# Loading v and z as fp32 through SyncE's queue and casting them on chip, in a gated attention and hypermixer kernel

## The chip, the cores and the metric

The kernel runs on one core of one Trainium2 chip. The metric is the device time of one execution in microseconds; a kernel is timed in several runs, and the median is given. A profiled execution of its own gives the trace and the page of views.

## The reference

Two stages follow each other, for 8 batches of 3200 rows:

```python
# u, v: (8, 3200, 256); z: (8, 3200, 64); w_q, w_k: (256, 64); w_out: (256, 256)
scores = (1.0 / S) * np.matmul(z, z.transpose(0, 2, 1))
attn = np.maximum(scores, 0.0) ** 2
x = u * np.matmul(attn, v)                       # the first stage
wq, wk = x @ w_q, x @ w_k                        # the second stage
W_tok = (1.0 / np.sqrt(64)) * np.einsum('bsd,btd->bst', wq, wk)
mixed = np.einsum('bst,btd->bsd', W_tok, x)
out = np.maximum(mixed, 0.0) @ w_out
```

All inputs and the output are fp32. The kernel multiplies in fp16.

## The kernel before, in words

**Tiling.** A batch is 25 blocks of 128 rows. The output rows of a batch are taken in seven groups (six of 512 rows and one of 128, `widths`). For each group and each of the 25 blocks, the scores are a 128 x 512 matrix: PE multiplies z with z (L263), two of these matrices making a pair in two PSUM banks (tile `sc`). A first stage on ACT or DVE takes the positive part into an fp32 tile `g` (`first_stage`, L286 and L290); a second stage on ACT or POOL squares it into the fp16 tile `at` (`second_stage`, L306 and L308). PE then multiplies `at` with the rows of v and adds up the group's output in four PSUM accumulators (`second_product`, tile `acc`, L351). At a group's end the two halves of the accumulators are added (L368, L369), multiplied with u on POOL (L388, tile `x_sb`) and transposed by a DMA (tile `xT_sb`).

**Symmetry.** The scores are symmetric, so a block that lies near the diagonal is computed once and its transposed copy is made by a DMA transpose from `at` into the tiles `tt` and `ttl` (L330).

**Second stage.** It is reordered so that no matrix of rows by rows is made: projections of x (L417, tile `qk`), a DMA transpose of the keys (tile `kx`), their product with x summed over the batch (`heads`, tile `ha`), the mix (`mix`, tile `mx`), its positive part (tile `rt`) and the product with w_out (`proj`, tile `fo`), which goes out by a DMA.

**What sets the order.** The program is emitted by hand, under a planner in the same file. It keeps a clock for each of PE, DVE, ACT and POOL, costs each piece of work with constants, and emits instructions in the order in which this plan runs them. `shut()` is the time at which the running group closes; `choose` and `squares` deal the two stages to engines by those clocks (`SPARE`, `BIAS`, `LATE`); `lead` says how many steps the scores run ahead of the products. Transfers on SyncE's queue are put down with `move(ready, due, issue, takes, fn, landed, may)` and taken by `flush` in order of their due time; `send` advances the plan's clocks of the queue (`sp_at`) and of the transfer engines (`dma_at`, `RING`, `LANDS`). A function `landed` says from which planned time the data may be used. Nothing of the plan exists at run time: each engine works through its list in order and waits by semaphores.

**v and z.** For the first batch, z comes as fp32 and is cast on chip, and v comes in four transfers of POOL's queue. For each later batch, `batch_begun` places one transfer of z (L156, into the fp16 tile `zn`) and five of v (L150, 5 blocks of rows each, into the fp16 tile `v_sb`) on POOL's queue; these transfers cast from fp32 to fp16 on their way. `v_sb` has two buffers, so batch b + 1 is loaded while batch b is used. z is then transposed by four DMA transposes (`turn_z`, L163), which are on SyncE's queue, as are all other loads, stores and transposes:

```python
def load_v(b, n0, nn):
    if n0 == 0:
        vs[b] = pv.tile([P, NT, D], FP16, tag="v_sb", name="v_sb")
    nc.gpsimd.dma_start(out=vs[b][:, n0 : n0 + nn, :], in_=rows(v, b)[:, n0 : n0 + nn, :])
```

Of the kernel before, what the change touches and what calls it, by code (L numbers as in the profile page):

```python
# [10 lines left out]
FP32 = mybir.dt.float32  # L11
# [5 lines left out]
def kernel(  # L17
# [48 lines left out]
    pg = ctx.enter_context(tc.tile_pool(name="pg", bufs=7))  # L66
# [80 lines left out]
    def load_v(b, n0, nn):  # L147
        if n0 == 0:
            vs[b] = pv.tile([P, NT, D], FP16, tag="v_sb", name="v_sb")
        nc.gpsimd.dma_start(out=vs[b][:, n0 : n0 + nn, :], in_=rows(v, b)[:, n0 : n0 + nn, :])  # L150
# [3 lines left out]

    def load_z(b):
        nc.gpsimd.dma_start(out=zn[:, 1 : NT + 1, :], in_=rows(z, b))  # L156
# [443 lines left out]
    MIXES = 10.0  # L600
# [9 lines left out]
    RING = 2.0  # L610
# [8 lines left out]
    def send(x):  # L619
# [4 lines left out]
        dma_at[0] = max(dma_at[0], begun) + takes  # L624
        sp_at[0] = max(begun + issue, dma_at[0] - RING)
        if landed:
            landed(max(sp_at[0], dma_at[0]) + LANDS)
# [67 lines left out]
    def squares():  # L695
        while pending and pending[0][0] <= clock[PE] + 0.3:
# [9 lines left out]
            for (b, gi, gj, _, nn, _, _), turn in second_stage(p, g, ways):  # L706
# [4 lines left out]
                    done + SLACK, due + SLACK, 1.28, 0.21 * n, turn,  # L711
# [6 lines left out]
    def block_landed(t, p, b, gi, gj, nn):  # L718
# [13 lines left out]
    def use_keys(b, gi):  # L732
# [17 lines left out]
        if not final:  # L750
            move(
                done + SLACK, done + 10.0, 1.28, 0.21 * n, lambda: turn_keys(b, gi),
                lambda t: at_time(t, lambda: double(b, gi)),
# [63 lines left out]
    def project_out(b, gi, ps, ready):  # L817
# [14 lines left out]
        move(done + SLACK, done + 6.0, 0.55, 1.6, stores[0], landed)  # L832

    def push(takes):
        give(POOL, clock[PE], 0.6)
        dma_at[0] = max(dma_at[0], clock[PE]) + takes

    Z0 = 24
    ZWAIT, ZDUE, ZSTEP, ZSTEP0 = 14.0, 32.0, 7.0, 5.0
    V0 = 56  # L840
    V1 = 10

    def batch_begun(b, t):
        if b + 1 < B:
            t0 = max(t + 6, Z0)
            at_time(t0, lambda: (load_z(b + 1), push(3.0)))
            step = ZSTEP if b else ZSTEP0
            for i, (_, m0, m1) in enumerate(ZTURNS):
                move(
                    t0 + ZWAIT + step * i, t0 + ZDUE + step * i, 1.28, 0.21 * (m1 - m0),  # L850
                    lambda i=i: turn_z(b + 1, i),
                    lambda t, i=i: z_ready.update({(b + 1, i): t}),
                )
# [321 lines left out]
```

## Time and profile before

| | |
|---|---|
| time, median of 3 runs | 775.03 us (774.68, 775.03, 778.61) |
| time of the profiled execution | 773.15 us |
| its span, first to last instruction | 770.9 us |
| mean granted clock of PE | 0.997 |
| busy: PE, DVE, ACT, POOL | 761.7, 510.5, 561.2, 591.1 us |
| packets' time on the queues q1 (SyncE's) and q0 (POOL's), as a share of 16 engines' span | 85.0%, 14.8% |

PE is TensorE's matrix products and PEld its loading of weights, which runs beside them; DVE is VectorE, ACT ScalarE, POOL GpSimd and SP SyncE. Engines work at the same time, so their busy times don't add up. A row of a group of instructions reads: line, engine, operation, output and input tiles, shapes, count, then the group's busy time, the mean duration of one in ns, and the idle time of the engine just before them with what ended it. The chain of waits is followed back from the last instruction of the execution.

### The profile page before, as it was taken

To read this page: it belongs to the slowest core of one execution; us is meant where nothing else is said; L and a number is where in the kernel's file an instruction comes from. 1 tells how busy PE (TensorE), PEld (TensorE's weight loads), DVE (VectorE), ACT (ScalarE), POOL (GpSimd) and SP (SyncE) were. 2 spreads that over 40 slices of the span, in tenths; PEclk is the share of its full clock that TensorE was granted. 3 is DMA by queue.
4 is the path that set the end of the run, shared out by engine and by line. 5 is a ranking of instruction groups with operands and counts; after the bars stand their busy time and mean duration, and the time that the engine had idled before them with its cause. 6 is when DMAs were issued, how large, how long until landed. Compare 5 with 4: busy or idle time off the path is not lost.

```text
span 770.9 us, 28221 instructions
## 1 busy us (share of the span) xinstructions
PE 761.7 (99%) x12408; PEld 678.4 (88%) x12408; DVE 510.5 (66%) x537; ACT 561.2 (73%) x647; POOL 591.1 (77%) x496
## 2 busy tenths in 40 slices
PE   8999999999999999999999999999999999999996
PEld 7889998888898888989889988998889989898884
DVE  6775876675787566765677756765667476675645
ACT  7785876778758678875788677877777676777734
POOL 8796788789687778666778687887878887888740
PEclk9999999999999999999999999999999999999998
DMA  8999999999999999999899999999999998979625
GB/s 199 130 187 182 167 204 173 160 212 194 194 162 189 194 209 190 182 213 203 153 190 162 188 231 163 219 145 160 262 156 192 184 190 211 201 143 203 152 84 191
DMA packets 307114, 141.09 MB, mean 183 GB/s; under 512 B 285744, under 2 KB 288432, under 8 KB 306992
## 3 DMA queue, kind: packets, MB, share of 16 engines
q1 hardware_dynamic: 300224, 123.13, 85.0%
q0 software_dynamic: 6624, 15.98, 14.8%
q8 instruction: 97, 1.59, 0.9%
q14 instruction: 25, 0.20, 0.1%
q10 hardware_dynamic: 144, 0.20, 0.1%
HBM read 59.64 MB, written 26.21 MB: 111 GB/s over the span
## 4 chain that ended last, share of the span: by engine, by line
PE 94%; POOL 2%; DVE 1%; DMA 1%; ACT 1%; issue 1%; POOLq 0%; SPq 0%; DVEq 0%; ACTq 0%
PE acc L351 68%; PE sc L263 13%; PE fo L521 6%; PE qk L417 3%; PE qk L455 2%; POOL at L308 2%; PE mx L483 1%; DMA z<-in_z_dram 1%; POOL x_sb L388 1%; DVE g L290 0%; ACT g L286 0%; DVE fo L546 0%; DMA xT_sb<-x_sb 0%; PE hd L455 0%; ACT at L306 0%
## 5 line engine op out<-in xcount | busy, mean ns | idle before, releaser
L351 PE MATMUL acc<-v_sb,at 64*128 64x256 f16 x7344 | 504.7, 269 | 0.0
L308 POOL TENSOR_TENSOR at<-g 128x1024 f16<-128x1024 f32 (+1 forms) x218 | 402.3, 1859 | 71.6 <-ACT g L286 29.1
L351 PEld LDWEIGHTS <-at 64*128 64x128 f16 x7344 | 407.2, 94 | 48.1 <-issue 4.8
L290 DVE TENSOR_SCALAR g<-sc 128x1024 f32<-128x1024 f32 (+2 forms) x285 | 338.5, 1203 | 122.8 <-PE sc L263 114.3
L306 ACT ACTIVATE at<-g 128x1024 f16<-128x1024 f32 (+2 forms) x255 | 257.2, 1023 | 21.8 <-DVE g L290 17.8
L286 ACT ACTIVATE g<-sc 128x1024 f32<-128x1024 f32 (+2 forms) x186 | 183.2, 989 | 76.8 <-PE sc L263 75.0
L388 POOL TENSOR_TENSOR x_sb<-both,u_sb 128x512 f16<-128x512 f32 (+1 forms) x112 | 135.8, 1217 | 81.6 <-DVE both L369 77.7
L263 PE MATMUL sc<-zT 64*128 64x512 f16 x924 | 188.1, 375 | 1.4 <-DVE g L290 0.6
L351 PE MATMUL acc<-v_sb,tt 64*128 64x256 f16 x2272 | 163.4, 269 | 0.0
L351 PEld LDWEIGHTS <-tt 64*128 64x128 f16 x2272 | 126.2, 94 | 10.3
L369 DVE TENSOR_TENSOR both<-acc,both 128x512 f32<-128x512 f32 (+1 forms) x104 | 69.6, 670 | 21.4 <-ACT both L368 17.0
L263 PEld LDWEIGHTS <-zT 64*128 64x128 f16 x924 | 61.2, 94 | 7.6 <-issue 3.9
L368 ACT COPY both<-acc 128x512 f32<-128x512 f32 (+1 forms) x69 | 39.0, 565 | 38.7 <-PE acc L351 36.1
L546 DVE TENSOR_SCALAR fo<-fo 128x1024 f32<-128x1024 f32 (+1 forms) x28 | 32.4, 1166 | 46.6 <-PE fo L521 46.6
L509 ACT ACTIVATE rt<-mx 128x1024 f16<-128x1024 f32 x39 | 39.9, 1024 | 12.6 <-PE mx L483 12.1
L521 PE MATMUL fo<-wo,rt 128*128 128x256 f16 x386 | 46.6, 273 | 0.5 <-ACT rt L505 0.5
L521 PEld LDWEIGHTS <-rt 128*128 128x128 f16 x386 | 36.2, 98 | 8.4 <-issue 3.6
L431 ACT CAST qk<-qk 128x512 f16<-128x512 f32 (+1 forms) x47 | 25.3, 539 | 24.6 <-PE qk L455 20.0
L368 DVE COPY both<-acc 128x512 f32<-128x512 f32 (+1 forms) x35 | 23.6, 674 | 21.2 <-PE acc L351 19.9
L470 DVE TENSOR_TENSOR ha<-qk,ha 128x512 f32<-128x512 f32 x37 | 25.5, 689 | 14.4 <-ACT qk L431 14.1
L551 ACT ACTIVATE fo<-fo 128x1024 f32<-128x1024 f32 (+2 forms) x23 | 22.5, 978 | 16.5 <-PE fo L521 15.8
L417 PE MATMUL qk<-xT_sb,wqk 64*128 64x256 f16 (+1 forms) x404 | 32.3, 265 | 0.0
(55 smaller groups left out, 282.9 us busy)
## 6 DMA issues: line engine op xcount, KB each, us to landing
u_sb<-in_u_dram SPq DMA_DIRECT2D x48, 512.0 KB, 4.8
out_dram<-fo SPq DMA_DIRECT2D x46, 512.0 KB, 5.1
v_sb<-in_v_dram POOLq DMA_DIRECT2D x35, 320.0 KB, 6.0
zn<-in_z_dram POOLq DMA_DIRECT2D x7, 400.0 KB, 7.8
tt<-at SPq DMA_TRANSPOSE x143, 4.7
u_sb<-in_u_dram SPq DMA_DIRECT2D x8, 128.0 KB, 2.9
out_dram<-fo SPq DMA_DIRECT2D x4, 256.0 KB, 3.3
xT_sb<-x_sb SPq DMA_TRANSPOSE x56, 5.4
```

Source lines behind the costliest of these rows:

```text
L263: nc.tensor.matmul(out=sc[h][:, 0:gw] if banks else sc[:, h, 0:gw], lhsT=z_cols(b, h, ti * P, P), rhs=z_cols(b, h, gs, gw), start=True, st ...
L286: nc.scalar.activation(out=g[:, hs, 0:w], in_=part, func=RELU, scale=GSCALE)
L290: nc.vector.tensor_scalar(out=g[:, hs, 0:w], in0=part, scalar1=0.0, scalar2=GSCALE, op0=AOP.max, op1=AOP.mult,)
L306: nc.scalar.square(out=out, in_=g[:, hs, 0:w])
L308: nc.gpsimd.tensor_mul(out=out, in0=g[:, hs, 0:w], in1=g[:, hs, 0:w])
L351: nc.tensor.matmul(out=accs[half, r][:, ds((j % 2) * D, D)], lhsT=weights(b, gi, ti, j)[top(r), :], rhs=vs[b][top(r), ti, :], start=(first ...
L368: copy(out=both[:, 0 : n * D], in_=accs[half, 0][:, 0 : n * D])
L369: nc.vector.tensor_add(out=both[:, 0 : n * D], in0=accs[half, 1][:, 0 : n * D], in1=both[:, 0 : n * D])
L388: nc.gpsimd.tensor_mul(out=xs[b, gi][:, 0:n, :, r, :].rearrange("p n c d -> p (n c) d"), in0=both[:, 0 : n * D].rearrange("p (m d) -> p m ...
L417: nc.tensor.matmul(out=ps[:, r, 0 : n * P], lhsT=wqk[top(r), c, :, :].rearrange("p t h -> p (t h)"), rhs=xTs[b, gi][top(r), 0:n, c, :], st ...
L509: nc.scalar.activation(out=out, in_=part, func=RELU)
L521: nc.tensor.matmul(out=banks[r][:, ds(j * D, D)], lhsT=flat[:, ds((dc * n + j) * P, P)], rhs=wo[:, dc, :], start=(dc == 0 and j == 0), sto ...
```

## The change

For batches 1 to 7, z and v no longer come through POOL's queue. Ten parts a batch, one of z and nine of v, are loaded as fp32 on SyncE's queue. Five of them are put into places of v's next buffer that later parts fill (`slot`, in rows of the fp16 tile), and five into two extra staging tiles of the pool `pst` (3 and 2 blocks of rows). ACT or POOL then casts each part, in pieces of up to 3 blocks of v or 9 of z, into `v_sb` or `zn`. An entry of `PARTS` holds: is it v, the first block of rows, the number of blocks, the slot (none for a staging tile), and how many parts must have been cast before it may be sent. To make room, the tile `g` has six buffers in place of seven.

The planner's constants change as well. What waits for a transfer is planned for a later time: turned blocks by `TURNS`, keys by `KEYS`, casts by `CASTS`, the projections of x by a larger `XWAIT`, output tiles by `STORES`; the cost of a transfer has a fixed part and a smaller part by size; the scores may run further ahead (`lead`); and `SPARE`, `BIAS`, `LATE` and `MIXES`, which deal work to engines and space the mixes, have new values. As all orders come out of the plan, the instructions of every engine stand in another order than before.

```diff
-    pg = ctx.enter_context(tc.tile_pool(name="pg", bufs=7))
+    pst = ctx.enter_context(tc.tile_pool(name="pst", bufs=1))
+    pg = ctx.enter_context(tc.tile_pool(name="pg", bufs=6))
...
+    STAGES = (3, 2)
+    PARTS = [
+        (False, 0, 25, 12.5, 0),
+        (True, 0, 3, 6, 0),
+        (True, 3, 5, 15, 1),
+        (True, 8, 2, 11, 2),
+        (True, 10, 3, None, 0),
+        (True, 13, 2, None, 0),
+        (True, 15, 2, 21, 3),
+        (True, 17, 3, None, 5),
+        (True, 20, 2, None, 6),
+        (True, 22, 3, None, 8),
+    ]
+    def load_part(b, i):
+        is_v, n0, nn, slot, _ = PARTS[i]
+        if i == 0:
             vs[b] = pv.tile([P, NT, D], FP16, tag="v_sb", name="v_sb")
-        nc.gpsimd.dma_start(out=vs[b][:, n0 : n0 + nn, :], in_=rows(v, b)[:, n0 : n0 + nn, :])
...
+        nc.sync.dma_start(out=stage_of[b, i], in_=rows(what, b)[:, n0 : n0 + nn, :])
+
+    def cast_part(b, i, m0, m1, by_act):
+        is_v, n0, _, _, _ = PARTS[i]
+        copy = nc.scalar.copy if by_act else nc.gpsimd.tensor_copy
+        out = vs[b][:, n0 + m0 : n0 + m1, :] if is_v else zn[:, 1 + m0 : 1 + m1, :]
+        copy(out=out, in_=stage_of[b, i][:, m0:m1, :])
...
-    def load_z(b):
-        nc.gpsimd.dma_start(out=zn[:, 1 : NT + 1, :], in_=rows(z, b))
...
-    MIXES = 10.0
+    MIXES = 12.0
...
-    RING = 2.0
+    RING = 1.5
...
-                row_at[b, gj, starts[gi] // P + n] = t + 0.5
+                row_at[b, gj, starts[gi] // P + n] = t + TURNS
...
-                lambda t: at_time(t, lambda: double(b, gi)),
+                lambda t: at_time(t + KEYS, lambda: double(b, gi)),
...
+    VTIMES = [0, 4, 18, 23, 28, 34, 40, 46, 53, 60]
+    V0 = 0.75
+    CASTS = 6.0
+    KEYS = 3.0
+    TURNS = 3.5
+    STORES = 4.0
...
+        if b == 0:
+            nc.gpsimd.memset(zn[:, 0 : NT + 2 : NT + 1, :], 0.0)
+        t0 = max(t + Z1, Z0)
+        for i, (is_v, _, nn, _, after) in enumerate(PARTS):
+            at = t0 + VTIMES[i] * (1.0 if b else V0)
+            move(
+                at, at + 8.0, 0.45, 0.2 + 1.5 * nn * (D if is_v else dqk) / 1024,
+                lambda i=i: part_sent(b + 1, i),
+                lambda t, i=i: at_time(t + CASTS, lambda: part_landed(b + 1, i)),
+                lambda i=i, after=after: sent[b + 1] == i and cast[b + 1][0] >= after
+                and (not after or cast[b + 1][1] + SLACK <= clock[PE]),
+            )
...
-            for i in range(5):
-                at = t + 20 + 13 * i if b else V0 + V1 * i
-                at_time(at, lambda i=i: v_loaded(b + 1, 5 * i, 5))
...
-    SPARE = 0.5
-    BIAS = 0.2
+    SPARE = 0.1
+    BIAS = -0.2
     XDUE = 5.0
-    XWAIT = 2.0
-    LATE = 0.5
+    XWAIT = 11.0
+    LATE = 0.3
...
-    lead = 140
+    lead = 170
...
-                and (x[1] != "proj" or all(t + 2.0 <= now for t in stored[-2:]))
+                and (x[1] != "proj" or all(t + STORES <= now for t in stored[-2:]))
```

More of the change, by code (lines that the diff above doesn't have):

```diff
@@ L623, in send @@
         begun = max(sp_at[0], clock[PE])
-        dma_at[0] = max(dma_at[0], begun) + takes
         sp_at[0] = max(begun + issue, dma_at[0] - RING)
+        dma_at[0] = max(dma_at[0], begun + max(issue, 0.9)) + takes
         if landed:
-            landed(max(sp_at[0], dma_at[0]) + LANDS)
+            landed(dma_at[0] + LANDS)
     def add_extra(t, kind, fn):
@@ L830, in landed @@
                 stored[i] = t
[L832 to L836, printed above, removed]
+        move(done + SLACK, done + 6.0, 0.45, 1.7, stores[0], landed)
     Z0 = 24
-    ZWAIT, ZDUE, ZSTEP, ZSTEP0 = 14.0, 32.0, 7.0, 5.0
-    V0 = 56
-    V1 = 10
-    def batch_begun(b, t):
[L844 to L848, printed above, removed]
+    Z1 = 6
@@ L1020 @@
     at_time(V3, lambda: (load_first_v(4, 8), give(POOL, clock[PE], 0.6)))
-    move(10.0, 14.0, 0.55, 1.6, lambda: load_u(0, 0))
+    move(10.0, 14.0, 0.45, 1.7, lambda: load_u(0, 0))
     load_weights()
```

58 lines of the change are left out of this document (43 added, 15 removed).

## The prediction

> **What bounds the kernel now.** I read the page first (busy shares, then the chain of work that ended last), then busy time by stretch, then what TensorE waited for, and last the transfer queues, because the change is about transfers.
>
> ```profile
> span 770.9 us, 28221 instructions
> PE 761.7 (99%) x12408; PEld 678.4 (88%) x12408; DVE 510.5 (66%) x537; ACT 561.2 (73%) x647; POOL 591.1 (77%) x496
> ...
> PE 94%; POOL 2%; DVE 1%; DMA 1%; ACT 1%; issue 1%; POOLq 0%; SPq 0%; DVEq 0%; ACTq 0%
> ```
>
> TensorE (PE) is busy 99% of the span and makes 94% of the chain; no other engine is above 77%. The average hides the stages, so here is busy time by stretch (microseconds busy, instructions in brackets, then clock and DMA share):
>
> ```profile
> 0.00:8.00 8.00, 6.60 (x64) 5.46 (x64) 3.94 (x9) 3.80 (x7) 4.61 (x13) 1.00 0.75 204
> 8.00:22.00 14.00, 13.37 (x197) 10.48 (x198) 11.03 (x10) 11.88 (x15) 13.82 (x10) 1.00 0.78 174
> 22.00:60.00 38.00, 37.34 (x614) 33.22 (x610) 28.49 (x28) 29.80 (x33) 32.62 (x27) 1.00 1.10 163
> 60.00:100.00 40.00, 40.00 (x689) 38.24 (x686) 27.96 (x33) 28.84 (x34) 28.54 (x27) 1.00 1.18 170
> 100.00:300.00 200.00, 200.00 (x3306) 175.77 (x3304) 136.49 (x143) 145.54 (x164) 160.78 (x135) 1.00 1.07 193
> 300.00:500.00 200.00, 199.89 (x3295) 180.94 (x3292) 135.27 (x139) 151.32 (x173) 151.65 (x126) 1.00 1.06 189
> 500.00:700.00 200.00, 200.00 (x3303) 180.88 (x3300) 128.44 (x132) 150.90 (x172) 163.56 (x137) 1.00 1.02 185
> 700.00:748.00 48.00, 48.00 (x784) 41.63 (x782) 26.55 (x29) 29.37 (x36) 30.52 (x24) 1.00 0.66 146
> 748.00:771.00 23.00, 16.54 (x186) 11.77 (x182) 12.37 (x18) 9.73 (x20) 4.99 (x4) 0.91 0.44 161
> ```
>
> From 60 to 748 us PE has 0.11 us of idle time. Idle PE is found only in the first 8 us (1.4 us, before any product), from 8 to 22 us (0.63), from 22 to 60 us (0.66) and after 748 us (6.46, the last batch's end). Between 22 and 748 us, where all of the changed loads are, one wait of PE's is listed; the chain's first 30 us show what holds the start:
>
> ```profile
> PE sc L263 <- DVE g L290: 0.4, 1, 0.4
> ```
>
> ```profile
> 7.40 2.04 POOL at L308 x2
> ...
> 10.00 10.30 POOL at L308 x6
> ...
> 21.95 1.97 PE acc L351 x36
> ```
>
> So PE waits for no transfer of v or z now. The start follows POOL's squares from 7.4 to 20.3 us; afterwards the products follow each other at 1.97/36 = 54.7 ns, and the number of products is not changed. A span cannot shrink by much: the idle time outside the end is 0.63 + 0.66 + 0.11 = 1.4 us. Busy spans of PE are modelled, so short gaps may hide in them; that bound is soft by a microsecond or two.
>
> **The change part by part.** First the transfers, then the casts, then the new order.
>
> ```profile
> q1 hardware_dynamic: 300224, 123.13, 85.0%
> q0 software_dynamic: 6624, 15.98, 14.8%
> ```
>
> ```profile
> u_sb<-in_u_dram SPq DMA_DIRECT2D x48, 512.0 KB, 4.8
> ...
> v_sb<-in_v_dram POOLq DMA_DIRECT2D x35, 320.0 KB, 6.0
> zn<-in_z_dram POOLq DMA_DIRECT2D x7, 400.0 KB, 7.8
> ```
>
> *Engines' DMA work.* The 42 transfers that POOL issues (35 x 320 KB and 7 x 400 KB) go: 14.3 of the 15.98 MB of queue q0, whose packets take 14.8% of 770.9 = 114 us of the sixteen engines, so 102 us go. They return on SyncE's (SP's) queue q1 as 28.7 MB of fp32. At q0's own price per byte read (114/31.96 = 3.6 us per MB) that is 102 us again; at q1's mean, transposes included (655 us for 123.13 MB, 5.3 us per MB), 152 us. I take 102, since plain rows resemble q0's reads more than 2-byte transposes. q1 is unused for 15% = 116 us: 102 fits, 152 does not. On the path of PE: 0.
>
> ```profile
> L174 SPq DMA_DIRECT2D u_sb<-in_u_dram x56: 327/529/1814, 5.0 to 738.3; - x56
> ...
> L330 SPq DMA_TRANSPOSE tt<-at x143: 1231/1354/5576, 17.1 to 713.4; - x143
> ```
>
> *Issue.* SP gets 70 loads (10 a batch, for batches 1 to 7) in its order: 70 x 0.529 (median of u's loads) = 37 us, at least 23, at most 127 where the queue is full. SP's order also carries every transpose, so each load is passed on to the blocks behind it as a delay. Cover: the distance that the program order leaves. I counted PE's order in both programs at 54.7 ns per product of 256 columns. From the last score of a turned block to the first product that reads it lie 39.7 us (median) before, 46.7 after, least 12.8 and 16.4. From a group's last product to the use of its transposed x: 19.1 and 26.1 (median). From a score pair to the first use of its squares: 8.4 and 12.0. Keys alone get a little tighter at the least, 16.8 to 15.0, median 22.7 and 23.1. So each wait for a transfer has about 7 us more room, against what a load in front costs: 102/70 = 1.5 us on average, 2.9 for z's 0.82 MB.
>
> The Trainium skill ("DMA: Bandwidth & Descriptors", section Queues, rings and completion order) says that a DMA engine takes turns among the queues that have work for it, packet by packet. On one queue that turn-taking is lost and a transpose stands behind the whole load; that speaks against the change, and no row here shows it, since now the loads have a queue of their own.
>
> ```profile
> L308 POOL TENSOR_TENSOR at<-g 128x1024 f16<-128x1024 f32 x211 | 396.5, 1893 | 70.0 <-ACT g L286 29.1 <-DVE g L290 29.0 <-issue 9.6
> L306 ACT ACTIVATE at<-g 128x1024 f16<-128x1024 f32 x240 | 250.8, 1056 | 21.8 <-DVE g L290 17.8
> L286 ACT ACTIVATE g<-sc 128x1024 f32<-128x1024 f32 x175 | 178.8, 1023 | 75.0 <-PE sc L263 73.2 <-POOL kx L448 0.9 <-POOL hs L477 0.6
> L150 POOL DMA_DIRECT2D v_sb<-in_v_dram x35 | 20.7, 591 | 0.0
> L308 POOL TENSOR_TENSOR at<-g 128x512 f16<-128x512 f32 x5 | 5.2, 1040 | 0.0
> L551 ACT ACTIVATE fo<-fo 128x1024 f32<-128x1024 f32 x21 | 21.5, 1024 | 15.6 <-PE fo L521 14.8 <-DMA u_sb<-in_u_dram 0.8
> L368 ACT COPY both<-acc 128x512 f32<-128x512 f32 x63 | 36.8, 584 | 34.3 <-PE acc L351 31.7 <-PE sc L263 1.1 <-PE hd L455 1.0
> L124 ACT CAST zd<-z 128x512 f16<-128x512 f32 x1 | 0.6, 619 | 1.8 <-DMA z<-in_z_dram 1.8
> L124 POOL CAST zd<-z 128x512 f16<-128x512 f32 x1 | 0.6, 609 | 0.9 <-DMA z<-in_z_dram 0.9
> L997 DVE MEMSET zn<- 128x64 uint32 x1 | 0.1, 112 | 0.0
> ```
>
> *Casts.* In the program order 91 casts appear, 54 on ACT (21 of v with 512 columns, 21 with 768, 12 of z with 448 or 576) and 37 on POOL (14, 14, 9). The rows have 0.62 and 0.61 us for 512 columns; for 768 I take 0.82 on ACT (halfway to the 1.02 of 1024 columns) and 0.91 on POOL (in proportion), for z 0.6. ACT: 13.0 + 17.2 + 7.2 = 37 us. POOL: 8.5 + 12.7 + 5.4 = 27 us, less 42 issues of 0.591 = 25 us that go.
>
> *What is dealt anew.* The planner's constants move work too. ACT: 36 more first stages, 13 fewer squares, 20 more output scalings, 14 fewer activations of the mix (priced as a scaling), 26 fewer copies of sums: 36.8 - 13.7 + 20.5 - 14.3 - 15.2 = +14. POOL: 9 more squares of 1024 columns and 6 of 512, 17.0 + 6.2 = +23. So ACT comes to about 561 + 37 + 14 = 612 us (79%), POOL to 591 + 27 - 25 + 23 = 616 (80%), and DVE falls by what ACT took over. All stay far under PE's 762, so on PE's path: 0, as long as no cast stands in front of something PE needs at once.
>
> ```profile
> ACT both L368 <- PE acc L351: 36.1, 45, 8.1
> ...
> DVE g L290 <- POOL at L308: 3.3, 3, 2.0
> ```
>
> That cover is thinnest in two places. At a group's end ACT's copy frees the accumulator: ACT now sits idle before it in 45 cases, 36.1 us in all, so a cast of 0.6 to 0.8 us mostly falls into idle time. If one in four of ACT's 54 casts delayed it by half a cast, that is 54/4 x 0.4 = 5 us. And the buffers of the first stage go from 7 to 6, while POOL does more: DVE's wait for POOL's squares is 3.3 us now, and PE met it with 0.4. I take 0 for the first and +0.3 for the second, bounds 0 to 5 and 0 to 2.
>
> *Start and end.* A second clearing of z's edge rows now stands on POOL between its first two squares, on the start's chain: +0.1 (DVE's took 0.11; bounds 0 and 0.3). The first squares are split a little more, between POOL and ACT: -1 to +1, taken as 0. The tail's order is the same on PE but for one projection (16 products) that moves behind the last block of products; PE's sum there is unchanged: 0.
>
> *The sum*, against the profiled execution's 773.15 (span 770.9): -0.7 (half of the 1.4 us of idle, which more room should remove) + 0.3 + 0.1 = -0.3, so 772.9. The runs' median is 775.03, 1.9 above the profiled one, and one run is 778.61. Some of that excess should be late transfers, which more room takes away: -0.7 of it. Forecast 775.03 - 0.3 - 0.7 = **774.0 us**, its own range 771 to 777.
>
> A second rule would give more. The Trainium skill ("SBUF — State Buffer", section SBUF: two separate sides) says that a DMA issued by GpSimd starves of descriptors while VectorE holds their common port, and advises a hardware queue instead. By it v's loads (6.0 us from issue to landing for 320 KB, against u's 4.8 for 512) would land sooner; but no row has PE waiting for v, so by the trace it is worth nothing here.
>
> **The rivals.** *Slower: transposes stand behind loads (0.20).* For it: q1 is already at 85%, transposes' issue is held up to 5.6 us, and the share in the stretches from 22 to 100 us is above the later ones. It decides once the added work exceeds q1's free 116 us. Halfway between my two prices (4.45 us per MB) it is 128 us, 12 over, which PE must wait out: 775 + 12 = 787; where the excess is only local, in batch 0, some 4 to 8. Against it: q0's 102 us on the same sixteen engines go, and the order leaves 7 us more.
>
> *Slower: casts in front of evacuations (0.08)*, the 5 us above: 780. It decides when a cast starts just as a group closes, which PE would show as waits for ACT's copy.
>
> *Faster (0.15).* All 1.4 us of idle go, the split squares shorten the start's chain by 1, and the 1.9 us by which the runs exceed the profiled one go: 775.0 - 4.3 = 770.7. For it: every distance to a transfer grows. Against it: 12 us of the 13 us chain at the start are POOL's squares, and POOL gets no faster.
>
> *That the change does not do what it says* is excluded: the order has the 70 loads on SP and no v or z transfer on POOL after batch 0.
>
> **How the numbers follow.** A difference of 0.5% (3.9 us) is about what a measurement of this kernel can tell from no change. Forecast 0.57 (within), faster 0.15, slower 0.20 + 0.08 = 0.28. The range takes the forecast, most of the faster case and the smaller half of the slower ones: 769.5 to 783.
>
> **What would show it.** Right: PE idle from 60 to 748 us still under 1 us, q0 near 2% and q1 over 95% or, if contention went with q0, a little under; ACT near 612, POOL near 616. Wrong: waits of PE's load or products for tt, ttl, xT or v, or for ACT's copy of the sums; long idle of PE at the batches' starts; a start chain that ends well off 20 us.

## The result, and the profile after

The changed kernel takes 782.0 us (median of 6 runs, 780.8 to 786.0) against 775.06 for the kernel before on the same chip (6 runs, 774.5 to 778.6). The ratio is 1.0088, 95% interval 1.006 to 1.0117: slower by 0.9%, where the forecast was 774.0 and no change. Two runs of the experiments below were in a slower state of the chip, at 788.8 and 882.5 us; no median counts them. The profiled execution has a span of 779.9 us, 9.0 more than before, at a mean granted clock of 0.996 (0.997 before).

The page of the profile after: span, busy time by engine, queues, and the chain by engine.

```profile
span 779.9 us, 28407 instructions
PE 763.8 (98%) x12408; PEld 667.5 (86%) x12408; DVE 483.6 (62%) x530; ACT 595.4 (76%) x695; POOL 614.8 (79%) x509
...
q1 hardware_dynamic: 310304, 151.80, 98.3%
q0 software_dynamic: 576, 1.64, 1.1%
...
PE 91%; POOL 2%; DMA 2%; issue 2%; ACT 1%; DVE 1%; SPq 0%; POOLq 0%; ACTq 0%; DVEq 0%
```

PE has the same 12,408 products. It is no longer busy all the time: the same stretches as in the prediction, PE first.

```profile
60.00:100.00 40.00, 40.00 (x682) 36.23 (x678) 27.16 (x31) 32.70 (x39) 32.54 (x31) 1.00 0.99 189
100.00:300.00 200.00, 194.88 (x3184) 168.43 (x3180) 119.83 (x130) 150.11 (x175) 160.89 (x131) 0.99 1.07 206
300.00:500.00 200.00, 198.97 (x3280) 175.62 (x3276) 123.61 (x134) 158.51 (x187) 164.29 (x132) 1.00 1.08 208
500.00:700.00 200.00, 200.00 (x3297) 173.84 (x3295) 126.18 (x139) 158.86 (x181) 165.10 (x134) 1.00 1.05 205
700.00:748.00 48.00, 46.61 (x770) 42.03 (x767) 27.39 (x32) 32.08 (x36) 33.53 (x31) 1.00 0.69 130
```

5.12 us are idle from 100 to 300 us, 1.03 from 300 to 500 and 1.39 from 700 to 748, 7.5 in all where the kernel before had 0.11. The four largest rows of PE's waits after the start (total, times, longest):

```profile
PE qk L445 <- ACT g L314: 3.7, 1, 3.7
PE qk L483 <- POOL kx L476: 1.4, 1, 1.4
PE mx L511 <- POOL hs L505: 1.3, 1, 1.3
PE sc L291 <- ACT rtl L537: 1.0, 1, 1.0
```

None of them names a transfer, and none is for a copy of the sums. For what made ACT late at the first one, three timelines of the same 10 us (start, duration, engine, line; idle time before it and its releaser in brackets): ACT, SP and PE.

```profile
164.74 1.02 ACT L314 ACTIVATE g<-sc 128x1024 f32<-128x1024 f32 x1 [0.37 <-PE sc L291]
170.71 0.83 ACT L181 CAST v_sb<-st 128x768 f16<-128x768 f32 x1 [4.95 <-DMA st<-in_v_dram]
171.45 1.05 ACT L334 ACTIVATE at<-g 128x1024 f16<-128x1024 f32 x1
172.41 1.00 ACT L314 ACTIVATE g<-sc 128x1024 f32<-128x1024 f32 x1
```

```profile
159.23 4.13 SPq L428 DMA_TRANSPOSE xT_sb<-x_sb  x1
163.46 1.22 SPq L358 DMA_TRANSPOSE ttl<-at  x1
164.73 1.29 SPq L191 DMA_TRANSPOSE zT<-zn  x1
166.12 1.32 SPq L175 DMA_DIRECT2D st<-in_v_dram  x1
```

```profile
173.46 0.91 PE L445 MATMUL qk<-xT_sb,wqk 64*128 64x256 f16 x8 [3.72 <-ACT g L314]
```

Read from below. PE has a projection to do but no free PSUM bank; ACT's first stage at 172.41 would free one. ACT works through its list in order, and ahead of that stage stands a square and ahead of the square a cast, which waits 4.95 us for its load. The load landed 4.6 us after its issue, as the others do (median 4.5); it was late because SP could issue it only at 166.12. SP had been at one transpose after another, and the transpose of x alone held it for 4.13 us, 2.9 more than the median of 1.28. So a full SP list becomes a late load, the late load a cast that stands still at the head of ACT's list, and that a bank that PE doesn't get.

Slow issues are not new. The longest of the transposes of x, and of the turned blocks (min/median/max in ns), were no shorter before:

```profile
L400 SPq DMA_TRANSPOSE xT_sb<-x_sb x56: 1190/1295/4657, 35.7 to 754.5; - x56
...
L428 SPq DMA_TRANSPOSE xT_sb<-x_sb x56: 1195/1278/4134, 32.3 to 761.9; - x56
...
L358 SPq DMA_TRANSPOSE tt<-at x143: 1231/1269/5079, 16.6 to 715.4; - x143
```

The first row is of the kernel before, where a turned block's issue took up to 5.576 us. Of all 328 transposes, 24 took over 3 us to issue before and 14 after. What is new is that a load with a cast waiting for it can stand behind one.

The wait also costs more than itself. For 3.99 us no product starts, and behind that the granted clock of PE (third column from the right) is at half for 3.4 us:

```profile
169.00:174.00 5.00, 1.28 (x21) 1.02 (x18) 1.00 (x1) 3.29 (x5) 1.73 (x2) 0.96 1.05 199
174.00:177.00 3.00, 3.00 (x28) 2.21 (x26) 1.92 (x2) 2.04 (x4) 2.65 (x2) 0.50 0.96 334
```

Before, the clock from 169 to 177 us is 1.00, and 54 products run in the 3 us in which 28 do here. Half a clock for 3.4 us loses 1.7 us, so by this estimate the one wait is worth 5.6 of the 9.0 us.

The 1.0 us of PE's last row, at 461.7 us, is again a cast on ACT that waits for its load (1.89 us), here with no slow transpose just before the load's issue. At 136 us a late transpose of keys holds POOL; at 714.6 us a sum on POOL (L505) stands behind squares, with no transfer in it.

The waits of ACT and POOL for transfers after the first batch:

```profile
POOL kx L476 <- DMA kx<-qk: 10.8, 8, 2.9
POOL v_sb L181 <- DMA st<-in_v_dram: 7.9, 3, 5.4
ACT v_sb L181 <- DMA st<-in_v_dram: 7.7, 4, 5.0
```

Before, POOL waited 2.2 us for keys, and no engine for v. As a sum over the whole run I use PE's gaps: the times from one product's start to the next's, where they are over 0.3 us (normally they are about 0.05 to 0.11), between 22 and 745 us, taken from the trace. They come to 2.2 us before and 10.2 after. What a half clock costs is for the most part not in them.

### The profile page after: what moved, and what is told of

It is laid out like the page before. It is cut to its first block, busy times and chain, and to the rows that moved or that the text cites. A ratio compares the mean times of both kernels' runs of the same rounds, so it can differ in the third digit from the quotient of the medians.

```text
span 779.9 us, 28407 instructions
## 1 busy us (share of the span) xinstructions
PE 763.8 (98%) x12408; PEld 667.5 (86%) x12408; DVE 483.6 (62%) x530; ACT 595.4 (76%) x695; POOL 614.8 (79%) x509
## 3 DMA queue, kind: packets, MB, share of 16 engines
q1 hardware_dynamic: 310304, 151.80, 98.3%
## 4 chain that ended last, share of the span: by engine, by line
PE 91%; POOL 2%; DMA 2%; issue 2%; ACT 1%; DVE 1%; SPq 0%; POOLq 0%; ACTq 0%; DVEq 0%
PE acc L379 66%; PE sc L291 13%; PE fo L549 6%; PE qk L445 3%; PE qk L483 2%; POOL at L336 2%; PE mx L511 1%; DMA st<-in_v_dram 1%; DMA z<-in_z_dram 1%; DVE g L318 1%; ACT g L314 0%; DVE fo L574 0%; PE xtx L594 0%; ACT fo L579 0%; PE hd L483 0%
## 5 line engine op out<-in xcount | busy, mean ns | idle before, releaser
L336 POOL TENSOR_TENSOR at<-g 128x1024 f16<-128x1024 f32 (+1 forms) x235 | 425.9, 1828 | 71.8 <-DVE g L318 54.3
L379 PEld LDWEIGHTS <-at 64*128 64x128 f16 x7344 | 396.1, 94 | 57.6 <-issue 4.9
L318 DVE TENSOR_SCALAR g<-sc 128x1024 f32<-128x1024 f32 (+2 forms) x255 | 297.5, 1185 | 157.4 <-PE sc L291 148.4
L314 ACT ACTIVATE g<-sc 128x1024 f32<-128x1024 f32 (+2 forms) x216 | 215.9, 1008 | 68.6 <-PE sc L291 67.0
L334 ACT ACTIVATE at<-g 128x1024 f16<-128x1024 f32 (+2 forms) x242 | 242.0, 1023 | 6.9 <-DVE g L318 4.5
L397 DVE TENSOR_TENSOR both<-acc,both 128x512 f32<-128x512 f32 (+1 forms) x104 | 69.7, 670 | 19.9 <-ACT both L396 12.5
L396 DVE COPY both<-acc 128x512 f32<-128x512 f32 (+1 forms) x63 | 42.4, 673 | 44.4 <-PE acc L379 43.4
L579 ACT ACTIVATE fo<-fo 128x1024 f32<-128x1024 f32 (+2 forms) x43 | 40.7, 995 | 15.4 <-PE fo L549 14.9
L396 ACT COPY both<-acc 128x512 f32<-128x512 f32 (+1 forms) x41 | 23.1, 564 | 23.4 <-PE acc L379 20.4
L476 POOL COPY kx<-kx 128x128 f16<-128x128 f16 (+1 forms) x99 | 25.8, 289 | 10.8 <-DMA kx<-qk 10.8
L539 DVE TENSOR_SCALAR rt<-mx 128x1024 f16<-128x1024 f32 x17 | 20.8, 1224 | 20.7 <-PE mx L511 20.7
```

The lines of the kernel that those rows point to most:

```text
L314: nc.scalar.activation(out=g[:, hs, 0:w], in_=part, func=RELU, scale=GSCALE)
L318: nc.vector.tensor_scalar(out=g[:, hs, 0:w], in0=part, scalar1=0.0, scalar2=GSCALE, op0=AOP.max, op1=AOP.mult,)
L334: nc.scalar.square(out=out, in_=g[:, hs, 0:w])
L336: nc.gpsimd.tensor_mul(out=out, in0=g[:, hs, 0:w], in1=g[:, hs, 0:w])
L379: nc.tensor.matmul(out=accs[half, r][:, ds((j % 2) * D, D)], lhsT=weights(b, gi, ti, j)[top(r), :], rhs=vs[b][top(r), ti, :], start=(first ...
L396: copy(out=both[:, 0 : n * D], in_=accs[half, 0][:, 0 : n * D])
```

## The experiments

Three theories were set against each other. *Theory 1*: a cast that waits for its load holds ACT or POOL. *Theory 2*: the new order of instructions is worse by itself; any small change of the planner's constants deals nearly every engine's order anew, so one kernel's time is a draw. *Theory 3*: queue q1, or the transfer engines as a whole (3b), are too full, and transposes land late. Theory 1 came first; the others took this shape as the runs came in, so the earliest expectations say in their own words what their rival is. "Gaps" below is the sum just described, of the profiled execution; the ratio to the kernel before on the same chip stands with its 95% interval. The runs come from several chips; the median of the kernel before on them is 775.1 to 775.9 us.

| kernel | median us (lowest to highest, runs) | ratio | gaps us |
|---|---|---|---|
| before | 775.06 (774.5 to 778.6, 6) | 1 | 2.2 |
| after | 782.0 (780.8 to 786.0, 6) | 1.0088 (1.006 to 1.0117) | 10.2 |
| order_only | 783.8 (780.0 to 791.6, 4) | 1.0127 (1.0061 to 1.0193) | 8.5 |
| loads_only | 782.4 (780.7 to 783.8, 4) | 1.0095 (1.0066 to 1.0125) | 8.9 |
| casts_pool | 776.1 (773.0 to 777.6, 10) | 1.0001 (0.9976 to 1.0026) | 3.9 |
| casts_late | 800.7 (799.7 to 802.5, 4) | 1.0341 (1.0312 to 1.037) | 22.8 |
| cast_fixed | 778.4 (773.2 to 783.5, 10) | 1.0035 (1.0003 to 1.0067) | 5.6 |
| no_staged_loads | 773.4 (772.6 to 775.4, 10) | 0.997 (0.9948 to 0.9991) | 2.2 |
| before_lead141 | 779.2 (777.6 to 780.7, 10) | 1.0041 (1.0015 to 1.0067) | 6.5 |
| before_mix | 776.8 (774.5 to 782.7, 10) | 1.0024 (0.9998 to 1.005) | 5.0 |
| after_lead171 | 780.0 (776.6 to 783.3, 7) | 1.0066 (1.0039 to 1.0094) | 8.7 |
| after_mix | 780.5 (774.7 to 786.3, 9, and one of 788.8) | 1.0076 (1.0042 to 1.0109) | 3.3 |
| casts_pool_171 | 780.3 (776.9 to 786.4, 6) | 1.0075 (1.0035 to 1.0114) | 8.0 |
| loads_actq | 821.3 (819.5 to 831.5, 4) | 1.0626 (1.0555 to 1.0697) | 47.6 |
| loads_poolq | 780.6 (775.9 to 784.1, 9, and one of 882.5) | 1.006 (1.0028 to 1.0092) | 13.1 |
| before_6g | 775.0 (773.0 to 782.6, 10) | 0.9995 (0.9964 to 1.0026) | 1.9 |
| staged_by_pool | 775.7 (771.9 to 777.6, 12) | 0.9984 (0.9959 to 1.0009) | 2.5 |
| staged_by_pool_171 | 773.7 (771.3 to 776.9, 10) | 0.9958 (0.9927 to 0.9989) | 1.3 |
| staged_by_pool_mix | 776.4 (774.0 to 777.9, 10) | 0.9997 (0.9975 to 1.0019) | 4.4 |

A profile is one execution: the one of after_mix (774.7 us) is its fastest run, those of loads_poolq (784.1) and before_mix (779.3) are among their slowest. In the latter the granted clock is at half for 6.8 us from 8.3 us on, which the profiles of before and after do not have, so not all that sets one execution apart from another need come from the order.

### One half of the change at a time

**order_only**: the changed planner's constants and rules, with the loads of before (POOL's queue, cast on the way) and 7 buffers of `g`.

```diff
-    pst = ctx.enter_context(tc.tile_pool(name="pst", bufs=1))
-    pg = ctx.enter_context(tc.tile_pool(name="pg", bufs=6))
+    pg = ctx.enter_context(tc.tile_pool(name="pg", bufs=7))
...
-        nc.sync.dma_start(out=stage_of[b, i], in_=rows(what, b)[:, n0 : n0 + nn, :])
+        nc.gpsimd.dma_start(out=vs[b][:, n0 : n0 + nn, :], in_=rows(v, b)[:, n0 : n0 + nn, :])
...
+    def load_z(b):
+        nc.gpsimd.dma_start(out=zn[:, 1 : NT + 1, :], in_=rows(z, b))
```

> The changed planner constants and order rules (later use of turned blocks, keys, x and output tiles, lead 170, new dealing), but v and z loaded as before, by casting transfers on POOL's queue, and seven buffers of the first stage. Theory 1 (a cast that is late with its own load holds its engine's list, and what frees PSUM stands behind it): without casts there is nothing to hold, PE's waits at 169 and 461 us of the changed kernel are gone, 772 to 776 us. Theory 2 (the new order and dealing alone cost the time, for example more work on ACT): 780 to 784 us. Theory 3 (SP's queue is overfull and everything on it is late): as theory 1, but with the keys' waits on POOL also gone.

**loads_only**: the new loads and casts under the constants of before.

```diff
-    MIXES = 12.0
+    MIXES = 10.0
...
-    KEYS = 3.0
-    TURNS = 3.5
-    STORES = 4.0
+    KEYS = 0.0
+    TURNS = 0.5
+    STORES = 2.0
...
-    XWAIT = 11.0
-    LATE = 0.3
+    XWAIT = 2.0
+    LATE = 0.5
```

> The new loads and casts, but the planner's old constants: nothing that waits for a transfer is placed later, old dealing, lead 140. Theory 1: late casts as in the changed kernel or more of them, 780 us or above, with ACT or POOL idle in front of casts. Theory 2 (new order costs the time): near 775 us. Theory 3: above the changed kernel, 785 us or more, since the old order leaves about 7 us less for each turned block while the queue carries the loads; PE then waits for turned blocks or keys.

Measured 783.8 and 782.4: either half alone costs as much as both, so they don't add up. In order_only no engine waits for v, but POOL waits for keys, with none of the new loads on SP's queue:

```profile
POOL kx L448 <- DMA kx<-qk: 28.5, 11, 5.7
```

PE's two largest gaps there are 2.3 us, at 354 us, for which the profile names no cause, and 2.1, where the sum on POOL stands behind squares. In loads_only the largest one, 3.4 us at 43 us, is the weights' cast on POOL (L233) standing behind u's products and squares, with no load in it. No cast waits for its load in loads_only, so what Theory 1 forecast for it is not there; PE waits a little for transposes of x (0.8 us in two waits), as Theory 3 had it, though its 785 or more did not come. Both halves had been given a new order by the way: Theory 2 had to be taken seriously, and the next comparisons had to keep the order.

### Where the casts run, and how late

**casts_pool**: `by_act = False`, so all 91 casts go to POOL (which deals the order anew). **casts_late**: every cast is planned 6 us later.

```diff
-            by_act = a + SPARE < c and (a + t_act <= shut() + LATE or a + 2.5 < c)
+            by_act = False
```

```diff
-    CASTS = 6.0
+    CASTS = 12.0
```

> The changed kernel with every cast on POOL and none on ACT. POOL holds no PSUM bank. Theory 1: ACT's idle time in front of casts is gone, and with it PE's two waits for PSUM banks (about 5.3 us of idle PE); waits move to POOL, where the squares stand behind them with 6 to 12 us of room: 775 to 778 us. Theory 2 or 3: no gain, 781 to 785 us, because POOL then carries 37 + 37 us more and the queue is as late as before.

> The changed kernel with the planned time from a load's landing to its cast raised from 6 to 12 us. Theory 1: the casts no longer find their load missing, ACT's and POOL's idle time in front of casts (7.7 and 7.9 us in the changed kernel) falls below 2 us, PE's waits at the two casts go, 775 to 778 us. Theory 2: 781 to 783 us. Theory 3: the casts' waits shrink but PE's waits for keys stay, and the time falls by no more than 3 us.

casts_pool took 776.1, as Theory 1 had it; casts_late 800.7, which no theory had. No cast waits there for its load any more, but casts of v come too late for the next batch, as PE's largest waits show:

```profile
PE acc L379 <- POOL v_sb L181: 8.7, 3, 3.5
PE qk L483 <- POOL kx L476: 5.0, 1, 5.0
PE qk L445 <- DMA xT_sb<-x_sb: 3.8, 1, 3.8
```

A part may be sent only when the part before it in its buffer has been cast (`after`), so I read this as delays that add up along the ten parts; that was not tried by itself. Whether 776.1 was POOL against ACT or a good draw, the same edit in another deal was to tell:

**casts_pool_171**: as casts_pool, and `lead` 171 for 170.

> All casts on GpSimd, as in the kernel that took 776.1, and the order dealt anew (lead 171 for 170). If a cast on ScalarE is what costs (ScalarE's first stages free PSUM, GpSimd's squares do so one step later): 775 to 778 again. If 776.1 was a good draw: 779 to 783.

780.3, with a gap of 2.6 us behind an output tile on ACT that waited 3.2 us for a store. With ACT's casts the same deal takes 780.0 (after_lead171, below), so the edit that gained 5.9 us in one deal gains nothing in the other, and 776.1 can't be put down to POOL.

### The same order, with the wait taken away, then the loads

**cast_fixed** keeps every engine's order; the casts of the five staged parts read a fixed tile of zeros and wait for no load, so that 13 of v's 25 blocks are zeros. The loads into the staging tiles are still made, but no longer wait for the cast of what a tile held (SP waits 3.4 us for casts in the changed kernel). **no_staged_loads** leaves these loads out too. What zeros alone do to the time was not tried; staged_by_pool, further below, computes all values.

```diff
-        copy(out=out, in_=stage_of[b, i][:, m0:m1, :])
+        if PARTS[i][3] is None:
+            half = 2 * (m1 - m0)
+            copy(
+                out=out.rearrange("p n (h d) -> p (n h) d", h=2),
+                in_=fixed[:].unsqueeze(1).to_broadcast([P, half, D // 2]),
+            )
+        else:
+            copy(out=out, in_=stage_of[b, i][:, m0:m1, :])
```

```diff
+        if slot is None:
+            return
         nc.sync.dma_start(out=stage_of[b, i], in_=rows(what, b)[:, n0 : n0 + nn, :])
```

> The changed kernel, with the order of every engine kept as it is. Only the casts of the five staged parts of each batch (rows 10 to 14 and 17 to 24 of v, 128-row blocks) read a fixed tile of zeros instead of the staging tile, so they wait for no load; the loads into the staging tiles are still made, and these blocks of v in the output's computation are zeros. Theory 1 (a cast that waits for its load at the head of ScalarE's or GpSimd's list holds what frees PSUM behind it): PE's gaps at 169.5 us (3.99) and 461.4 us (1.30) go, 5.3 us less: about 776.5, span 774.6; the gaps of the keys (136, 1.6) and of the squares (714.6, 1.6) stay. Theory 2 (the new planned order is worse by itself, wherever the casts stand): 780 to 782, other gaps in place of these. Theory 3 (queue q1 is too full, so transposes land late): 780 to 782, since q1 carries the same bytes.

> As the one with fixed casts, and in addition the five staged loads of each batch (35 in all, of 128x1024 or 128x1536 fp32) are not made, so q1 carries about 23 MB less and SyncE issues 35 loads fewer; the same blocks of v are zeros. Theory 1: as with fixed casts within 1 us, about 776. Theory 3 (q1 too full): the wait of the keys' doubling at 136 us and SyncE's long busy stretches go too, 773 to 775, and clearly less than with fixed casts (by 2 us or more). Theory 2: both stay at 780 to 782.

Both theories, 1 and 3, had a share. In one order, 782.0 became 778.4 without the waits of the staged casts (3.6 us less) and 773.4 without their loads (another 5.0). The profiled spans, one execution each, split the same sum another way: 779.9, 774.6 and 772.7. In cast_fixed the gaps at 169 and 461 us are gone as Theory 1 said. That its span is the 774.6 us forecast is in part luck: the gap at 136 us went too, and two new ones came, 1.5 us at 83 us, where PE waits for a transpose of z, and 2.0 at 446 us. In the second a part that isn't staged does what the staged ones did (ACT, then SP, of cast_fixed):

```profile
445.30 0.62 ACT L189 CAST v_sb<-v_sb 128x512 f16<-128x512 f32 x1 [2.35 <-DMA v_sb<-in_v_dram]
445.83 1.05 ACT L342 ACTIVATE at<-g 128x1024 f16<-128x1024 f32 x1
446.78 1.92 ACT L587 ACTIVATE fo<-fo 128x1024 f32<-128x1024 f32 x2
```

```profile
437.73 4.59 SPq L436 DMA_TRANSPOSE xT_sb<-x_sb  x1
442.37 0.57 SPq L176 DMA_DIRECT2D v_sb<-in_v_dram  x1
```

Again a transpose of x holds SP (4.59 us), the load behind it is issued late, and its cast holds ACT's output tiles, for which PE waited 1.7. In no_staged_loads no engine waits for z, v or keys after the first batch, q1 stands at 88.1%, and the ten runs lie within 2.8 us, against 10.3 in cast_fixed. The gap of the sum behind squares on POOL (1.56 us, at 708) stays in both: it belongs to this order, not to the transfers.

### How much a new deal of the order does

**before_lead141** (`lead` 141 for 140), **before_mix** (`MIXES` 10.5 for 10.0), **after_lead171** (171 for 170), **after_mix** (12.5 for 12.0).

> The kernel before with one of the planner's constants changed by a hair (lead 141 for 140), which deals nearly every engine's order anew and changes no amount of work. Theory 1 and 3 (the loads and casts cost the time): 775 as before, within 1.5 us. Theory 2 (each order is a draw, and the one before was a good one): 777 to 784, with gaps of PE of 1 to 3 us that before does not have.

> A second new deal of the order before (MIXES 10.5 for 10.0), with the same loads that cast on the way and the same work. Theory 2 (each order is a draw; the one before was a good one): 776 to 781, as with lead 141 (779.2), with 4 to 8 us of PE's gaps from 22 to 745 us. If the new deal with lead 141 was an exception: 775 within 1 us.

> The changed kernel with one of the planner's constants changed by a hair (lead 171 for 170), which deals nearly every engine's order anew and changes no amount of work. Theory 1 (late casts are in any order a risk): 778 to 784, with a few gaps of PE of 1 to 4 us at other places, the largest behind a cast that waits for its load. Theory 2 (each order is a draw): anywhere from 774 to 786, and its gaps need not be at casts. Theory 3 (q1 too full): 780 or more, gaps at transposes.

> A second new deal of the changed order (MIXES 12.5 for 12.0). If the loads and casts on the chip cost time in any order: 779 to 784, with 7 to 11 us of PE's gaps from 22 to 745 us, at least one of them behind a cast that waits for its load. If the changed order was merely a bad draw: as likely below 778 as above.

Before in three deals: 775.1, 779.2, 776.8, mean 777.0. After in three: 782.0, 780.0, 780.5, mean 780.8. Theory 2 is right in this: the kernel before was a good draw by some 2 us, and one deal against another is worth up to 4. It is not the whole cause. In after_lead171 the largest gap (3.0 us) is again a cast at nearly the same time, this time with the sums' copy behind it (ACT and DVE):

```profile
170.84 0.83 ACT L181 CAST v_sb<-st 128x768 f16<-128x768 f32 x1 [3.91 <-DMA st<-in_v_dram]
171.58 0.58 ACT L396 COPY both<-acc 128x512 f32<-128x512 f32 x1
...
172.19 0.69 DVE L397 TENSOR_TENSOR both<-acc,both 128x512 f32<-128x512 f32 x1 [4.68 <-ACT both L396]
```

In after_mix the forecast time came but not the forecast gaps of 7 to 11 us: its profile has 3.3, though ACT's casts wait 6.4 us for loads in it. Set beside order_only (783.8), which has the old loads, three deals a side alone would not settle it. A comparison within the same deal does, and follows.

### The loads on another queue

**loads_actq** and **loads_poolq** issue the 70 loads from ACT's and from POOL's list, casts and bytes as they are, the other engines' orders kept.

```diff
-        nc.sync.dma_start(out=stage_of[b, i], in_=rows(what, b)[:, n0 : n0 + nn, :])
+        nc.gpsimd.dma_start(out=stage_of[b, i], in_=rows(what, b)[:, n0 : n0 + nn, :])
```

> The changed kernel with the 70 loads of v and z issued on ScalarE's list instead of SyncE's; the order of TensorE, VectorE and GpSimd is kept as it is, and so are all casts and all bytes. Theory 1 with its cause in SyncE's list (a load is issued late because transposes in front of it fill the queue, and its cast then holds ScalarE or GpSimd): ScalarE pays 70 issues, about 37 us by the median of u's loads (0.53), at 76% busy; casts no longer wait 4 to 5 us for their loads and keys are turned sooner, so 776 to 779. Theory 3b (it is the bytes on the sixteen engines, not the one queue): 781 to 784, casts wait as before. Rival: ScalarE waits in the place of SyncE when a load's buffer is not free or the queue is full, and holds the first stages behind it: 785 or more.

> The changed kernel with all 70 loads of v and z, still as fp32 into the same places and cast on the chip in the same places, issued on GpSimd's list, so on q0. The order of TensorE, VectorE and ScalarE is kept. GpSimd pays 70 issues of about 0.59 us, 41 us, and stands at 84%. If the one queue is the cause (loads and transposes held behind each other): casts wait for their loads less than 1 us each and it is 775 to 779. If it is the bytes: casts wait as before and 781 to 784. Rival, as with the loads on ScalarE's list (821.3): GpSimd waits at an issue whose buffer is not free yet and holds squares behind it: 785 or more.

On ACT it took 821.3: ACT stood still in front of issues (9 us around one at 64.7 us), with everything that frees PSUM behind them; PE waited 23.5 us for its first stages. On POOL the casts wait for nearly nothing (0.6 us), as the queue theory said, and it is still 780.6. PE's one large gap (6.7 us at 84 us) has its cause in transposes: POOL waits for a buffer of `at` that a transpose still reads,

```profile
87.56 3.74 POOL L336 TENSOR_TENSOR at<-g 128x1024 f16<-128x1024 f32 x2 [12.17 <-DMA ttl<-at]
```

and in the 20 us around it (68 to 88 us) two loads took 9.5 and 11.8 us to land and the turned blocks between them 12.1, by the table of transfers (engine, count, size, median to landing):

```profile
st<-in_v_dram POOLq DMA_DIRECT2D x1, 384.0 KB, 9.5
...
st<-in_v_dram POOLq DMA_DIRECT2D x1, 256.0 KB, 11.8
...
tt<-at SPq DMA_TRANSPOSE x2, 12.1
```

So another queue takes the casts' waits away, and transfers of both queues can still land late together; why they did here the trace doesn't show, and one gap in the one profiled execution (784.1 us) doesn't account for the median. The Trainium skill ("DMA: Bandwidth & Descriptors", section Queues, rings and completion order) says that engines take turns between queues packet by packet. The prediction took this to protect a transpose from loads on another queue; here turned blocks with two loads beside them on the other queue took 12.1 us, against a median of 4.3 in the changed kernel.

**staged_by_pool** puts only the five staged parts back: the transfer casts on its way and is issued by POOL where the cast stood, so nothing waits at the head of a list. z and the four parts staged in `v_sb` stay as changed, and so does the order.

```diff
+        if slot is None:
+            at = slice(n0 + m0, n0 + m1)
+            return nc.gpsimd.dma_start(out=vs[b][:, at, :], in_=rows(v, b)[:, at, :])
         copy = nc.scalar.copy if by_act else nc.gpsimd.tensor_copy
```

**staged_by_pool_171** and **staged_by_pool_mix** are the same in the deals of after_lead171 and after_mix.

> The changed kernel's order, and all of the reference is computed; but the five staged parts of each batch (35 transfers) go back to GpSimd's queue as transfers that cast on the way, each issued where its cast stood, so there is no staging tile and no cast for them. Their bytes are read again, by queue q0 instead of q1. Theory 1+3 (the loads make SyncE's queue late, and casts and transposes wait for it): PE's gaps at 136, 169 and 461 us go, q1 falls to some 88%, 773 to 776, within 2 us of the run without the staged loads (773.4). Theory 3b (it is the bytes on the sixteen engines): 778 to 782. Theory 2 (the order): 780 to 782, gaps at new places.

> The same with the order dealt anew (lead 171 for 170). If the staged loads on SyncE's queue are the cause in any order: 774 to 777. If one order's luck: 778 to 782, as the changed kernel with lead 171 (780.0).

> A third deal of the order (MIXES 12.5 for 12.0) with the five staged parts of each batch on GpSimd's queue, cast on the way. The changed kernel took 780.8 in this deal. If the staged loads on SyncE's queue with their waiting casts are the cause in any order: 773 to 777, as in the two deals run so far (775.7 and 773.7). If those two were good draws: 778 or more.

| deal | after | staged parts back on POOL's queue | difference |
|---|---|---|---|
| the changed kernel's | 782.0 | 775.7 | -6.3 |
| `lead` 171 | 780.0 | 773.7 | -6.3 |
| `MIXES` 12.5 | 780.5 | 776.4 | -4.0 |

In three orders the same step brings 4.0 to 6.3 us. The page of staged_by_pool shows PE back at 99%, and q1 at 91.5%:

```profile
span 770.7 us, 28402 instructions
PE 761.2 (99%) x12408; PEld 672.3 (87%) x12408; DVE 483.4 (63%) x530; ACT 582.5 (76%) x672; POOL 625.4 (81%) x532
...
q1 hardware_dynamic: 305264, 139.87, 91.5%
q0 software_dynamic: 5616, 7.60, 7.8%
```

No cast waits for its load in it, and keys wait 4.2 us in place of 10.8. staged_by_pool_171 is the one version that beats both kernels (ratio to before 0.9958, 0.9927 to 0.9989), but 0.4% is no more than a good deal gives; the mean of the three, 775.3, is 1.8 below before's three deals, which these runs can't tell from a difference of draws.

### The first stage's buffers

**before_6g**: the kernel before, order kept, with 6 buffers of `g`.

> The kernel before, order and work kept, with 6 buffers of the first stage in place of 7. Prices one term of the prediction: +0.3 us, bounds 0 to 2, so 775.0 to 777.0. Theory 2 has no say, since the order is the same. If the buffers were a cause of the loss: 778 or more, with PE waiting for VectorE's or ScalarE's first stages.

775.0, no change: this part of the change costs nothing.

## Why the prediction was wrong

**What held.** PE bounds the kernel, and the products are the same. The signs that the prediction named for its being wrong did not show: PE waited for no turned block, no x, no v after the first batch, and not for ACT's copy of the sums. The sign for its being right, under 1 us of idle PE from 60 to 748 us, did not show either: it is 7.5. The packets' time was priced well: q1's took 98.3% of 779.9 = 767 us against 655 before, 111 more where 102 was forecast. The casts' execution came out at 37.5 us on ACT and 25.9 on POOL (37 and 27 forecast), POOL's total at 614.8 (616), SP's 70 issues at 39 us by their medians (37). ACT's total was 595 instead of 612, since its instructions overlap at their ends: their durations add up to 634 us, 47 more than before where 51 were forecast, and the busy time rose by 34. That costs nothing either way. The buffers of `g` cost nothing (+0.3 forecast), and the idle time from 8 to 60 us hardly moved (1.2 us after, 1.3 before).

**The step that failed** is "All stay far under PE's 762, so on PE's path: 0, as long as no cast stands in front of something PE needs at once", and the count behind it: a cast was priced by its execution, 0.6 to 0.9 us, also in the rival that had casts in front of evacuations. What the runs showed in its place is the cast's own wait: 91 new instructions that each depend on a transfer were put into two lists that are worked through in order. A wait of 4.95 us on an engine that is 76% busy went into PE's time at 3.7, and the half clock behind it cost another 1.7 by the estimate above. The casting transfer of before had no such wait. The staged casts' waits were worth 3.6 us by the medians (782.0 to 778.4). The rival's own form, a cast in front of ACT's copy of the sums, is what after_lead171 shows in another order.

**The step beside it** was "102 fits". It compared a queue's share of the engines' time with what was left to 100%. But q0 and q1 together stood at 99.8% before and stand at 99.4% after, and from 68 to 88 us the profile of before has 98.0% and 27.2% side by side: such a share does not measure room. What the timelines show at the gaps is SP's list: SP stood 4 to 5 us at a transpose of x, as it had before, and now a load with a cast waiting for it came next. This is the rival "transposes stand behind loads" turned round: what came late first were the loads and the keys, behind transposes. Its local size of 4 to 8 us fits, by another mechanism, so that the agreement is luck; and that 782.0 lies within the stated range is owed to the rivals that the range took in, not to the sum. The staged loads were worth 5.0 us (778.4 to 773.4). The distances counted in PE's order grew by the prediction's count, which no run measures, but they covered turned blocks, x and squares; the distance that decided, from a load's issue to its cast, was new and was not counted. The keys' distance was the one that shrank, and their wait went from 2.2 to 10.8 us. The loads are not its only cause: it is 0 in the same order without the staged loads, but 28.5 in order_only, which has none of the new loads.

**What the prediction did not see at all** is that before was a good draw among orders, some 2 us better than the mean of three. The 0.7 us that more room was to take from the runs' excess can't be judged: the median of the runs is now 0.3 above the profiled execution (781.7) in place of 1.9, but that execution is itself 8.5 us longer.

The Trainium skill's other rule ("SBUF — State Buffer", section SBUF: two separate sides), by which v's loads are better off GpSimd's queue, did not decide here: with the staged parts back on it, and their casts gone, the kernel is 4.0 to 6.3 us faster in each of three orders. No run takes the queue apart from the cast.

**What stays open.** How the 5.0 us divide between SP's in-order list and the transfer engines' load is known only roughly. staged_by_pool moves the staged parts by another queue, with the queues' shares again at 99.3% together, and takes 775.7, between 778.4 and 773.4; that speaks for SP's list in about half of it. But all loads on POOL's queue, which frees SP's list of them too, took 780.6. Why order_only takes 783.8 is open as well: it is one deal, of four runs that lie 11.6 us apart, and its largest gap has no cause in the profile. A version with the loads on a queue that blocks no compute engine was not tried.

## What to carry to other kernels

A cast on chip in place of a casting transfer costs more than its 0.8 us: it puts a wait for a transfer at the head of an in-order list, so list what stands behind it and who needs that, and count the distance from its load's issue, not only from its data's use. Judge a queue by what stands behind its slowest instruction, not by its mean share: transposes took up to 5.6 us to issue before, and it cost nothing until loads that a cast waits for stood behind them. Where a planner deals every order from its constants, run a few harmless variations of both kernels, or keep the order fixed, before a difference below 1% is put down to an edit.

## What was not expected of the hardware

- A stall of PE cost more than itself once it was long enough. Between 22 and 745 us the nineteen traces have 18 distances of 2.3 us or more from one product's start to the next's; in or within 2.1 us behind all of them but one (2.94 us, in loads_actq), the granted clock is at half for 3.4 us or a multiple of it. Behind none of the 18 distances of 1.2 to 2.2 us is it.
- The spread of a kernel's runs does not follow its queue's share: 2.8 us with q1 at 88.1% (no_staged_loads), 3.0 at 83.9% (before_lead141) and 10.3 at 96.4% (cast_fixed), but 11.6 in four runs at 86.2% (order_only). The longer runs tend to have the lower granted clock: before_6g's run of 782.6 has 0.993, its others 0.996 to 0.999.
- The issue of a transpose on SP, 1.3 us as a rule, took up to 5.6 us before and 5.1 after, and delayed what stood behind it on the list.
- The same 70 loads cost 39 us more when ScalarE issued them than when SyncE did (821.3 against 782.0), though one issue took ScalarE only 0.34 us: ScalarE stood still in front of them.
